# Retention, experts and a max-of-three layer on one core: weight loads, splits and clearing moved between stages

## The chip, the core and the metric

The kernel runs on one core of a Trainium2 chip. The metric is device time in microseconds (us). TensorE is called PE in the rows, VectorE DVE, ScalarE ACT, GpSimd POOL and SyncE SP; SPq and ACTq are the queues from which these engines issue transfers.

## The reference

Retention over 4 batches, 8 heads, 576 positions and 64 dimensions gives 2304 rows of 512 numbers. A gate sends each row to one of 8 experts (1024 wide, capacity 576), whose result is scaled by the gate's weight. A last layer takes the largest of three products and multiplies it by an output matrix.

```python
scores = scale * np.matmul(q, k.transpose(0, 1, 3, 2))
ret = scores * Dmat[None]                      # gamma[h] ** (i - j) for i >= j, else 0
x = np.matmul(ret, v)                          # rows of all heads: [2304, 512]
expert_idx = np.argmax(x @ w_gate, axis=1)     # softmax of the logits gives gate_w
# disp[e, counts[e]] = x[i] for the first `capacity` rows of an expert
h = np.maximum(np.einsum('ecd,edf->ecf', disp, w1), 0.0)
y = np.einsum('ecf,efd->ecd', h, w2)
out[i] = gate_w[i] * y[expert_idx[i], pos[i]]
h = np.maximum(np.maximum(out @ m2_w1, out @ m2_w2), out @ m2_w3)
return h @ w_out
```

## The kernel before

**Three stages.** The program has an order written out by hand; each engine runs its instructions in that order, and semaphores join the engines. The stages are retention with the gate (0 to 133 us of the profile), the eight experts (133 to 373 us) and the last layer.

**Retention.** The 2304 rows go in 20 chunks of 128 rows (every fifth has 64). Step `t` of the loop over chunks works on several chunks at once: PE computes the scores of chunk t+1 (`scores`, L270), turns chunk t-1 and gives its gate logits (`transposes`, L491), adds to the running state (`update`, L295) and computes the outputs of chunk t (`outputs`, L315 and L327). DVE reduces the logits of chunk t-1 (L382 in chunks 0 to 13, L344 later), masks the scores (`cut`, L276), scales the outputs (L336) and the v rows of a chunk two or three ahead (`vprime`, L254). ACT copies the turned rows to a row buffer `xg` (`take`, L389), which frees the one PSUM bank that `transposes` fills. A row buffer waits there for its gate weights. Chunks 0 to 13 are gated in three groups (5, 5, 4): after the group's last chunk `group_choose` picks the experts, `group_place` (PE, L427 on) counts places, and `group_send` scales each row buffer (L483) and writes it to `xd` in DRAM from ACT's queue (L484). Only then is the buffer free; there are seven.

**Loads.** SP issues chunk loads `qk` and `kv` (512 KB each, five and six buffers) up to six chunks ahead, and in the same queue the expert weights (`load_unit`, L138, three buffers `raw` of 512 KB), and at step 4 four writes that put zeros into rows of `xd` (L728). Each transfer that SP or ACT issues takes one of eight completion semaphores in turn; its issue waits until the transfer eight places before it has landed.

**Units.** A unit is 128x1024 weights. `split_hi` (ACT, L144) rounds it to a high part and `split_lo` (DVE, L149) takes the rest; that frees its `raw`. Each expert has eight units: four for the first product (`mm1`), four for the second (`mm2`), one per output block `d`. Before, five units are split in retention (`SPLIT_AT`, high part at the end of that step, low part at the end of the next) and the others in the experts, where `next_split` splits one and loads the next.

**Outputs table.** `spread_otab` (L664) spreads decay factors over partitions by four products with a 0/1 matrix `sel`, which ACT makes first (L702).

**The sum y.** `y` is 128x4x2656 numbers. POOL clears it (L1223 before the first expert, L1092 in the step after its first output block). `mm2` writes each output block into it (ACT, L1144).

## Time and profile before

| what | value |
|---|---|
| median of 3 runs | 668.2 us (661.24 to 670.61) |
| profiled execution | 665.12 us, span 663.1 us, mean granted clock 0.984 |
| PE busy | 634.7 us (96%) |
| DVE busy | 440.1 us (66%) |
| ACT busy | 277.2 us (42%) |
| POOL busy | 215.5 us (33%) |
| bytes moved | 124.05 MB, mean 187 GB/s |

How to read it: PE is busy nearly all the time, so a change pays only where PE waits or runs at the lower of its two clock levels. "Busy" counts a slow matmul as busy, so a stretch with PE at 100% and a granted clock of 0.50 has lost half of its time. The two levels are 2.4 GHz (1.00) and 1.2 GHz (0.50).

### The profile page before, as it was taken

What the parts mean: (1) busy time and instruction counts of PE and PEld (TensorE: products, weight loads), DVE (VectorE), ACT (ScalarE), POOL (GpSimd) and SP (SyncE); (2) the same over time, 40 slices, a digit from 0 to 9 for tenths busy, and PEclk for the clock granted to TensorE, in tenths of its full rate; (3) what the DMA queues carried; (4) which work ended last, traced back from release to release, by engine and by line L of the source; (5) the groups of instructions that cost most, each with busy time, mean ns of one, the idle gap of its engine ahead of it and who ended that gap; (6) DMA issues with size and microseconds to landing.
All of it is one profiled execution on the core that took longest, in us unless ns stands there. A gap on an engine that the chain in (4) does not pass through costs nothing. (4 is left out here: it accounts for less than half of the span.)

```text
span 663.1 us, 12029 instructions
## 1 busy us (share of the span) xinstructions
PE 634.7 (96%) x4523; PEld 596.4 (90%) x4523; DVE 440.1 (66%) x869; ACT 277.2 (42%) x504; POOL 215.5 (33%) x188
## 2 busy tenths in 40 slices
PE   8999989899999999999989999999999999999995
PEld 5888877799999999898979999997899998999983
DVE  3478757774857578689697556577887677446630
ACT  2336324444656565555646543433522225221221
POOL 1001121255655745278885044540210002100011
PEclk8999968999999999999999999999999999999998
DMA  8889952255678787777866324357889641544011
GB/s 280 275 268 324 306 165 104 82 131 184 199 209 223 214 245 208 237 221 239 235 234 207 124 74 136 95 179 263 268 268 316 210 132 49 163 138 146 30 48 50
DMA packets 69876, 124.05 MB, mean 187 GB/s; under 512 B 18506, under 2 KB 41422, under 8 KB 69816
## 3 DMA queue, kind: packets, MB, share of 16 engines
q1 hardware_dynamic: 51896, 94.62, 45.8%
q0 software_dynamic: 15520, 24.50, 12.2%
q10 hardware_dynamic: 2400, 4.14, 1.8%
q8 instruction: 37, 0.61, 0.4%
q14 instruction: 23, 0.19, 0.1%
HBM read 97.27 MB, written 25.91 MB: 186 GB/s over the span
## 5 line engine op out<-in xcount | busy, mean ns | idle before, releaser
L149 DVE TENSOR_TENSOR w<-raw,w 128x1024 fp32r<-128x1024 f32 x72 | 99.9, 1389 | 44.7 <-ACT w L144 44.6
L1138 PE MATMUL b<-h,w 128*128 128x336 f32 (+7 forms) x768 | 118.5, 307 | 3.0 <-DVE h L1114 1.6
L1138 PEld LDWEIGHTS b<-h,w 128*128 128x128 f32 x768 | 109.0, 188 | 5.7 <-DVE h L1114 2.5
L144 ACT ACTIVATE w<-raw 128x1024 fp32r<-128x1024 f32 x72 | 75.9, 1055 | 25.4 <-DMA raw<-in_weights_dram 24.0
L1460 POOL DMA_INDIRECT out_dram<-o,perm_sb x18 | 20.0, 1110 | 192.2 <-ACT o L1458 160.0
L1098 PE MATMUL a<-xt,w 128*128 128x336 f32 (+7 forms) x256 | 77.6, 303 | 0.9 <-DVE xt L196 0.9
L1097 PE MATMUL a<-xt,w 128*128 128x336 f32 (+7 forms) x256 | 77.7, 304 | 0.0
L1099 PE MATMUL a<-xt,w 128*128 128x336 f32 (+7 forms) x256 | 77.3, 302 | 0.0
L187 POOL DMA_INDIRECT who_d<-tok,slots_i x20 | 22.7, 1135 | 100.3 <-DMA who_d<-tok,slots_i 62.2
L1098 PEld LDWEIGHTS a<-xt,w 128*128 128x128 f32 x256 | 48.2, 188 | 1.2 <-DVE xt L196 1.2
L1097 PEld LDWEIGHTS a<-xt,w 128*128 128x128 f32 x256 | 48.1, 188 | 0.5 <-ACT xt L195 0.5
L174 POOL DMA_INDIRECT xr<-xd,who x24 | 37.1, 1547 | 34.8 <-DVE order_w L1159 16.2
L1099 PEld LDWEIGHTS a<-xt,w 128*128 128x128 f32 x256 | 48.1, 188 | 0.0
L1494 PE MATMUL s<-b_ys,w 128*128 128x384 f32 x216 | 40.7, 335 | 1.6 <-ACT p L1524 1.6
L1097 PE MATMUL u<-ys,w 128*128 128x384 f32 x126 | 42.1, 334 | 0.0
L1098 PE MATMUL u<-ys,w 128*128 128x384 f32 x126 | 42.1, 334 | 0.0
L1099 PE MATMUL u<-ys,w 128*128 128x384 f32 x126 | 42.1, 334 | 0.0
L1494 PE MATMUL s<-b_xt,w 128*128 128x384 f32 x216 | 40.4, 334 | 0.0
L1494 PE MATMUL s<-b_h,w 128*128 128x384 f32 x216 | 40.3, 334 | 0.0
L1494 PEld LDWEIGHTS s<-b_ys,w 128*128 128x128 f32 x216 | 37.6, 188 | 2.2 <-ACT p L1524 1.9
L1113 ACT ACTIVATE h<-a 128x336 fp32r<-128x336 f32 (+7 forms) x64 | 26.6, 422 | 29.8 <-PE a L1099 29.6
L1494 PEld LDWEIGHTS s<-b_xt,w 128*128 128x128 f32 x216 | 37.8, 188 | 0.2
(287 smaller groups left out, 1329.1 us busy)
## 6 DMA issues: line engine op xcount, KB each, us to landing
raw<-in_weights_dram SPq DMA_DIRECT2D x64, 512.0 KB, 5.2
w<-sd SPq DMA_DIRECT2D x68, 256.0 KB, 4.1
kv<-in_kv_dram SPq DMA_DIRECT2D x16, 512.0 KB, 5.9
qk<-in_qk_dram SPq DMA_DIRECT2D x15, 512.0 KB, 7.3
d<-in_weights_dram POOLq DMA_DIRECT2D x14, 512.0 KB, 5.9
sd<-y SPq DMA_DIRECT2D x13, 512.0 KB, 3.2
wdec<-mag POOLq DMA_DIRECT2D x16, 256.0 KB, 3.8
raw<-wdec SPq DMA_DIRECT2D x8, 512.0 KB, 3.7
```

Of the source, the lines that this page charges most:

```text
L144: act.activation(out=t[:, 0], in_=raws[w], func=AF.Copy)
L149: engine.tensor_tensor(out=t[:, 1], in0=raws.pop(w), in1=t[:, 0].bitcast(F32), op=ALU.subtract)
L174: pool.indirect_dma_start(out=xr[:n, r, :], out_offset=None, in_=xd[:, :], in_offset=bass.IndirectOffsetOnAxis(ap=who[:n, r, e : e + 1] if ...
L187: pool.indirect_dma_start(out=who_d[:, :], out_offset=bass.IndirectOffsetOnAxis(ap=slots_i[:L, t : t + 1], axis=0), in_=tok[:L, t : t + 1] ...
L1097: pe.matmul(ps, lhsT=wh, rhs=xh, start=first, stop=False)
L1098: pe.matmul(ps, lhsT=wh, rhs=xl, start=False, stop=False)
L1099: pe.matmul(ps, lhsT=wl, rhs=xh, start=False, stop=last)
L1113: act.activation(out=h[:, 0, :wide], in_=ps, func=AF.Relu)
L1138: pe.matmul(ps, lhsT=w[:, a, f * P : (f + 1) * P], rhs=hs[f][:, b, :wide], start=(i == 0), stop=(i == len(todo) - 1),)
L1460: pool.indirect_dma_start(out=out[:, :], out_offset=bass.IndirectOffsetOnAxis(ap=perm_sb[:, g : g + 1], axis=0), in_=o, in_offset=None,)
L1494: pe.matmul(ps, lhsT=a[:, k], rhs=b[:, c], start=first and c == 0 and n == 0, stop=c == 1 and n == 2, skip_group_check=True,)
```

## The change

- Loads: eight units are loaded in retention in both versions. Before, `raw` loads are issued at steps 2, 4 and 5 and behind low parts; now one at each of the steps 2, 3, 5, 6, 7, 10, 11, 12.
- Splits: high parts at steps 4, 6, 7, 8, 9 before, and at 4, 5, 8, 9, 10, 12, 13, 14 now. Eight units, a whole expert, are split in retention, three more than before. The first expert's `mm1` splits one unit instead of three. In the experts 1, 3 and 4 `mm1` splits four units instead of five; the experts 1 and 3 split two behind their last output block.
- Three `raw` loads of the second expert are issued ahead of the first expert's work.
- The zeros of `xd` are written at step 13 instead of 4.
- Eight row buffers `xg` instead of seven, in the room of `sel`. `spread_otab` takes a broadcast column of the identity in `cst` instead, in eight products of 64 columns instead of four of 128.
- ACT clears `y`, one block in each of the steps 0, 2, 8 and 9 of the first expert; POOL clears nothing.

```diff
--- before.py
+++ after.py
@@ -49,9 +49,11 @@
 NCHUNK = len(CHUNKS)
 NPOS = -(-S // P)
 NPATCH = 3
-LOAD_AT = [2, 4, 5]
-SPLIT_AT = [4, 6, 7, 8, 9]
+LOAD_AT = [2, 3, 5, 6, 7, 10, 11, 12]
+SPLIT_AT = [4, 5, 8, 9, 10, 12, 13, 14]
+ZERO_AT = 13
 EARLY_SCATTER = 10
+CLEAR_AT = [0, 2, 8, 9]
 TRANS_AT = [(0, 23), (1, 11), (1, 23), (2, 11)]
 TRANS_FIRST = [(2, 14), (2, 22), (3, 6), (3, 14)]
 GROUPS = [range(0, 5), range(5, 10), range(10, 14)]
@@ -365,7 +367,7 @@
                 dve.reciprocal(out=g[:L], in_=g[:L])
                 ix_t[t], oh_t[t], g_t[t] = ixf, oh, g
                 if NCHUNK - NPATCH <= t < NCHUNK - 1:
-                    xg_t[t] = wk.tile([P, DM], F32, tag="xg", name=f"xg{t}", bufs=7)
+                    xg_t[t] = wk.tile([P, DM], F32, tag="xg", name=f"xg{t}", bufs=8)
                     act.activation(
                         out=xg_t[t][:L].rearrange("p (c n) -> p c n", c=NC), in_=xps_t[t][:L, :, :P], func=AF.Copy
                     )
...
@@ -655,16 +657,18 @@
             dve.memset(ones, 1.0)
 
             decs = st.tile([H, S], F32, name="decs")
-            sel = st.tile([H, NPAIR, 2, D], F32, name="sel")
 
             def spread_otab(j):
                 a, n = j * P, min(P, S - j * P)
                 bank = ps_1.tile([P, DM], F32, tag="po", name=f"spread{j}")
                 for r in range(NPAIR):
-                    pe.matmul(
-                        bank[:, r * n : (r + 1) * n], lhsT=sel[:, r].rearrange("h a d -> h (a d)"),
-                        rhs=decs[:, a : a + n], start=True, stop=True,
-                    )
+                    for par in range(2):
+                        h = 2 * r + par
+                        pe.matmul(
+                            bank[par * D : par * D + D, r * n : (r + 1) * n],
+                            lhsT=ident[:H, h : h + 1].to_broadcast([H, D]),
+                            rhs=decs[:, a : a + n], start=True, stop=True,
+                        )
                 act.activation(
                     out=otab[:, :, a : a + n], in_=bank[:, : NPAIR * n].rearrange("p (r n) -> p r n", r=NPAIR),
                     func=AF.Copy,
@@ -699,11 +703,6 @@
                 skip_group_check=True,
             )
             vprime(1)
-            act.activation(
-                out=sel,
-                in_=ident[:H, :H].rearrange("h (r a) -> h r a", a=2).unsqueeze(3).to_broadcast([H, NPAIR, 2, D]),
-                func=AF.Copy,
-            )
             spread_otab(0)
             for lg_ in lgs:
                 pool.memset(lg_, 0.0)
@@ -720,7 +719,7 @@
                     sp.dma_start(out=cat[:, A_SEQ:], in_=consts[:, C_KEEP + A_SEQ :])
                 if t == 0:
                     act.dma_start(out=who_d.rearrange("(p c) o -> p (c o)", p=P), in_=zero)
-                if t == 4:
+                if t == ZERO_AT:
                     tail = sum(L for _, _, L in CHUNKS[NCHUNK - NPATCH :])
                     blocks = [(0, 1)]
                     blocks += [(r, min(P, 1 + NTOK - r)) for r in range(1 + NTOK - tail, 1 + NTOK, P)]
@@ -797,8 +796,6 @@
                     sent.setdefault(t + 1, []).append(GROUPS[i][j])
                 if t - 1 in SPLIT_AT:
                     split_lo(nxt["split"] - 1, dve)
-                    if nxt["load"] < 8:
-                        next_load()
                 if t < NPOS - 1:
                     spread_otab(t + 1)
                 if t == 0:
@@ -1074,8 +1071,14 @@
         ready = {at - 1: n for n, at in enumerate(slots)}
         slots = {at: n for n, at in enumerate(slots)}
 
+        def clear(c):
+            blank = nc.const_aps.tensor(0.0, [P, NTOK + max(WIDTH)], F32)
+            act.activation(out=y[:, c], in_=blank, func=AF.Copy)
+
         def dec_step(e, k):
             at = e * LAST + k
+            if at in CLEAR_AT:
+                clear(CLEAR_AT.index(at))
             if unsent and at >= LAST and at % 3 == 0:
                 scatter(unsent.pop(0), due=True)
             if (e, k) in finds:
@@ -1087,9 +1090,6 @@
                 decode_top(slots[at + 1])
             if at in slots:
                 decode(slots[at])
-                if slots[at] == 0:
-                    for c in range(NC // 2, NC):
-                        pool.memset(y[:, c], 0.0)
             if at in ready:
                 dec_act(ready[at])
 
@@ -1118,9 +1118,8 @@
                 h_t[e, f] = h
                 if f % 2:
                     units.pop(8 * e + f // 2)
-                if f % 2 or (e in (1, 3, 4) and f == 4):
-                    if (e, f) != (0, 1):
-                        next_split()
+                if f == F // P - 1 or (e and f % 2):
+                    next_split()
                 dec_step(e, f)
 
         def mm2(e):
@@ -1144,7 +1143,8 @@
                 act.activation(out=y[:, d, bass.ds(off, wide)], in_=ps, func=AF.Copy)
                 if e == E - 1:
                     ysplit_part(0, d)
-                next_split()
+                for _ in range(2 if e in (1, 3) and d == NC - 1 else 1):
+                    next_split()
                 dec_step(e, F // P + d)
 
         def scratch(name):
@@ -1218,9 +1218,9 @@
         dec_load(0)
         dec_load(1)
         find_order()
+        for _ in range(3):
+            next_load()
         load_x(1)
-        for c in range(NC // 2):
-            pool.memset(y[:, c], 0.0)
         h2_t, ys_t, m2 = {}, {}, {}
 
         def ysplit_part(i, c):
```

SP's queue around steps 3 to 6 of retention, where the zeros and the raw loads stood (qk, kv: chunk loads; raw: a weight unit), before:

```order
L728 DMA xd_86<-zero_160 4x1x128
L728 DMA xd_86<-zero_160 512x1x128 x2
L728 DMA xd_86<-zero_160 256x1x128
L138 DMA raw1_447<-in_weights_dram 128x1024
L225 DMA qk9_500<-in_qk_dram 128x8x64
L231 DMA kv9_502<-in_kv_dram 64x1024
L138 DMA raw2_504<-in_weights_dram 128x1024
L138 DMA raw3_566<-in_weights_dram 128x1024
L225 DMA qk10_568<-in_qk_dram 128x1024
L231 DMA kv10_570<-in_kv_dram 128x1024
L225 DMA qk11_660<-in_qk_dram 128x1024
```

and now:

```order
L140 DMA raw1_405<-in_weights_dram 128x1024
L227 DMA qk7_455<-in_qk_dram 128x1024
L233 DMA kv7_457<-in_kv_dram 128x1024
L227 DMA qk8_459<-in_qk_dram 128x1024
L233 DMA kv8_461<-in_kv_dram 128x1024
L227 DMA qk9_514<-in_qk_dram 128x8x64
L233 DMA kv9_516<-in_kv_dram 64x1024
L140 DMA raw2_518<-in_weights_dram 128x1024
L227 DMA qk10_582<-in_qk_dram 128x1024
L233 DMA kv10_584<-in_kv_dram 128x1024
L140 DMA raw3_586<-in_weights_dram 128x1024
```

The four zeros are gone from here, and between two raw loads stand one to three chunks' loads; raw2 and raw3 no longer follow each other.

DVE at the end of step 14, between the third group's choice (gids) and the gate of chunk 14 (lg, mx, ix, oh), before:

```order
L414 TENSOR_TENSOR goh_1196<-gsame_1193,gtop_1192 128x32
L415 TENSOR_TENSOR gids_1197<-goh_1196,tab_124 128x64
L344 TENSOR_REDUCE lg_1221<-xps_1216 64x8
L351 MAX mx_1223<-lg_1221 64x8
L353 MAX_INDEX ix_1225<-mx_1223,lg_1221 64x8
L360 CAST ixf_1232<-ix_1225 64x1
L362 TENSOR_SCALAR oh_1234<-cst,ixf_1232 64x8
```

and now:

```order
L416 TENSOR_TENSOR goh_1219<-gsame_1216,gtop_1215 128x32
L417 TENSOR_TENSOR gids_1220<-goh_1219,tab_124 128x64
L151 TENSOR_TENSOR w_1156<-raw_937,w_1156 128x1024
L346 TENSOR_REDUCE lg_1247<-xps_1242 64x8
L353 MAX mx_1249<-lg_1247 64x8
L355 MAX_INDEX ix_1251<-mx_1249,lg_1247 64x8
L362 CAST ixf_1258<-ix_1251 64x1
L364 TENSOR_SCALAR oh_1260<-cst,ixf_1258 64x8
```

One low part (w<-raw,w) has come in ahead of the gate; the same has happened at the ends of steps 13 and 15.

ACT behind the first two output blocks of the first expert (y<-b: an output block; w<-raw: a high part; xt<-tp: the next expert's rows; ISA: register work), before:

```order
L1144 ISA
L1144 ACTIVATE y<-b_0_1992 128x336
L144 ACTIVATE w_2018<-raw_1892 128x1024
L1144 ISA
L1144 ACTIVATE y<-b_1_2032 128x336
L144 ACTIVATE w_2058<-raw_1938 128x1024
L195 ACTIVATE xt_2079<-tp_0_2080 128x352
```

and now:

```order
L1143 ISA
L1143 ACTIVATE y<-b_0_2015 128x336
L146 ACTIVATE w_2041<-raw_1857 128x1024
L1076 ACTIVATE y<-const-float32-0.0 128x2656
L1143 ISA
L1143 ACTIVATE y<-b_1_2054 128x336
L146 ACTIVATE w_2080<-raw_1859 128x1024
L1076 ACTIVATE y<-const-float32-0.0 128x2656
L197 ACTIVATE xt_2102<-tp_0_2103 128x352
```

Behind each of the first two output blocks ACT now clears a block of y; two more clears stand behind the hidden blocks 0 and 2 of `mm1`, and two high parts that stood there are gone.

## Rows read from the trace of the kernel before

In the timelines a row gives start and length in us, engine, line, operation, out<-in, shapes and number, and in brackets the idle time before it and what ended it. In the windows PE, its weight loads, DVE, ACT and POOL stand in that order.

**Rows 1.** The page: granted clock of PE in 40 slices of 16.6 us.

```profile
PEclk8999968999999999999999999999999999999998
```

**Rows 2.** Windows, steps 6, 11, 13, 14, 15: length; engines busy; clock; DMA share; GB/s.

```profile
44.76:50.08 5.32, 5.32 (x70) 4.71 (x69) 4.82 (x20) 2.15 (x5) 0.77 (x1) 1.00 0.79 276
70.85:76.31 5.46, 5.46 (x69) 4.73 (x68) 4.80 (x20) 2.14 (x5) 0.78 (x1) 1.00 1.01 352
79.63:86.58 6.95, 4.94 (x56) 4.18 (x56) 2.54 (x6) 1.92 (x3) 0.90 (x1) 0.94 1.04 365
86.58:94.89 8.31, 8.31 (x74) 7.74 (x76) 3.60 (x13) 1.58 (x4) 1.92 (x2) 0.50 0.57 168
94.89:102.42 7.53, 6.51 (x94) 5.53 (x91) 6.61 (x31) 2.76 (x7) 1.95 (x2) 0.93 0.10 21
```

**Rows 3.** Windows, three stretches of low clock, then one of transfers.

```profile
10.30:14.10 3.80, 3.80 (x48) 3.32 (x44) 1.89 (x3) 1.21 (x4) 0.00 (x0) 0.55 1.09 379
84.80:95.90 11.10, 10.87 (x99) 9.93 (x99) 4.66 (x19) 2.94 (x9) 1.92 (x2) 0.54 0.60 194
105.90:109.70 3.80, 3.79 (x24) 3.33 (x24) 2.72 (x10) 2.13 (x3) 0.00 (x0) 0.55 0.35 137
46.00:90.00 44.00, 39.83 (x513) 35.33 (x511) 32.59 (x85) 20.31 (x36) 5.75 (x5) 0.95 1.02 323
```

**Rows 4.** Timeline, PE in retention: start, length, instruction, idle before and releaser.

```profile
8.87 1.15 PE L664 MATMUL spread<-decs,sel 8*128 8x128 f32 x8 [1.07 <-ACT sel L702]
...
45.40 1.09 PE L327 MATMUL o<-pt,vp 128*64 128x128 f32 x16
...
58.31 1.19 PE L491 MATMUL xps<-idw,xT 128*128 128x136 f32 x8 [0.94 <-ACT xg L389]
...
69.57 0.17 PE L433 MATMUL gpo<-goh,tri 128*128 128x8 bf16 x1 [0.93 <-DVE goh L414]
...
85.03 1.51 PE L491 MATMUL xps<-idw,xT 128*128 128x136 f32 x8 [2.01 <-ACT xg L389]
```

**Rows 5.** Timeline, ACT in retention.

```profile
8.19 0.63 ACT L702 ACTIVATE sel<-cst 8x512 f32<-8x512 f32 x1 [5.95 <-DMA cst<-in_consts_dram]
...
84.38 0.60 ACT L389 ACTIVATE xg<-xps 128x512 f32<-128x512 f32 x1 [3.94 <-DMA xd<-xg]
```

**Rows 6.** Timeline, DVE in retention.

```profile
67.68 0.69 DVE L254 TENSOR_TENSOR vp<-kv,cat 128x512 f32<-128x512 f32 x1 [0.91 <-DMA kv<-in_kv_dram]
...
83.99 0.69 DVE L254 TENSOR_TENSOR vp<-kv,cat 128x512 f32<-128x512 f32 x1 [1.74 <-DMA kv<-in_kv_dram]
```

**Rows 7.** Timeline, SP's queue, step 5 of retention.

```profile
37.66 7.54 SPq L138 DMA_DIRECT2D raw<-in_weights_dram  x2
```

**Rows 8.** Waits of SP's queue in retention: us in total, times, longest.

```profile
SPq L231 <- DMA xd<-xg: 8.6, 2, 6.5
```

**Rows 9.** Timeline, PE in experts 0 to 4, its waits that the change touches.

```profile
166.62 0.43 PE L1098 MATMUL a<-xt,w 128*128 128x352 f32 x1 [0.91 <-DVE xt L196]
...
243.05 2.13 PE L1138 MATMUL b<-h,w 128*128 128x308 f32 x12 [0.58 <-ACT h L1113]
...
273.50 2.21 PE L1138 MATMUL b<-h,w 128*128 128x296 f32 x12 [0.87 <-ACT h L1113]
```

**Rows 10.** Timeline, POOL and ACT in experts 0 and 4.

```profile
161.09 4.61 POOL L1092 MEMSET y<- 128x2656 f32 x2
...
163.48 0.45 ACT L1144 ACTIVATE y<-b 128x336 f32 x1 [3.14 <-POOL y L1092]
...
268.16 1.06 ACT L144 ACTIVATE w<-raw 128x1024 fp32r<-128x1024 f32 x1 [3.48 <-DMA raw<-in_weights_dram]
```

**Rows 11.** Groups of instructions in retention: xcount, busy us, mean ns, idle before.

```profile
L149 DVE TENSOR_TENSOR w<-raw,w 128x1024 fp32r<-128x1024 f32 x5 | 6.1, 1215 | 0.0
...
L144 ACT ACTIVATE w<-raw 128x1024 fp32r<-128x1024 f32 x5 | 5.3, 1057 | 2.8 <-ACT xg L483 1.4 <-DMA raw<-in_weights_dram 1.4
```

**Rows 12.** The page: output blocks of the experts, 24 matmuls each.

```profile
L1138 PE MATMUL b<-h,w 128*128 128x336 f32 (+7 forms) x768 | 118.5, 307 | 3.0 <-DVE h L1114 1.6
```

More of the change, by code (lines that the diff above doesn't have):

```diff
@@ L387, in take @@
                 )
-                xg_t[t] = wk.tile([P, DM], F32, tag="xg", name=f"xg{t}", bufs=7)
+                xg_t[t] = wk.tile([P, DM], F32, tag="xg", name=f"xg{t}", bufs=8)
                 act.activation(
@@ L519, in gate2 @@
                 xps = xps_t.pop(t)[:L, :, :P]
-                xg = xg_t.pop(t) if t in xg_t else wk.tile([P, DM], F32, tag="xg", name=f"xg{t}", bufs=7)
+                xg = xg_t.pop(t) if t in xg_t else wk.tile([P, DM], F32, tag="xg", name=f"xg{t}", bufs=8)
                 if t < NCHUNK - NPATCH:
```

## The prediction

> **What bounds the kernel now.** I read the page first: PE is busy in 96% of the span, and its granted clock is well below full in two slices, 83 to 116 us, and a little in the first and the last [rows 1]. So a gain has to come from places where PE waits, or from a stretch at 1.2 GHz. Then I cut retention into windows by step, and the low stretches by themselves [rows 2, 3], and took PE's waits from its timeline, one by one [rows 4, 9]. For each wait I followed the releaser: to ACT [rows 5, 10], from there to a transfer or to POOL, and for late transfers to SP's queue [rows 6 to 8].
>
> What the reader is to see: in steps 6 and 11 PE is busy throughout, with DVE at 4.8 of 5.3 to 5.5 us close behind it. Step 13 takes 6.95 us with PE idle for 2.0 of them; the idle time is the wait at 85.03, ahead of `transposes`, for ACT's copy into a row buffer, and that copy waited 3.94 us for a row buffer's write to DRAM to land [rows 2, 4, 5]. Behind it PE falls to 1.2 GHz for 11.1 us and step 14 takes 8.31 us at a clock of 0.50, PE busy all the time [rows 2, 3]. From 133 us on the experts keep PE full but for a few waits of 0.6 to 0.9 us [rows 9].
>
> **The change, part by part.** Durations are of the profiled execution, 665.1 us (span 663.1 and 2.0 around it).
>
> 1. *No `sel`.* The first spread waits 1.07 us for `sel`, which ACT makes in 0.63 us once the constants have landed at 8.19 [rows 4, 5]. The constants are still needed, so 0.6 us goes. The spread itself becomes eight products of 64 columns. Bounds: the outputs' 64-column products come in pairs and take 1.09 us for 16 rows of the trace, the full-width spread 1.15 us for 8 [rows 4], so the price is nil; if the pairs ran one behind the other it would be 1.15 us more, five times at most, 5.5 us. I take nil, since the output products write the same two halves of the bank. **-0.6 us.**
>
> 2. *Eight row buffers.* Chunk 7 needs an eighth buffer before chunk 0's has landed in DRAM, chunk 12 before chunk 5's. The waits of 0.94 us at 58.31 and of 2.01 us at 85.03 end there [rows 4]. What is late next at 85: DVE waits 1.74 us for `kv` until 83.99 [rows 6]. That one goes only if item 3 holds. **-0.9 and -2.0 us.**
>
> 3. *Loads one by one.* SP's queue stood 7.54 us on two `raw` loads in a row, the second waiting for the low part that frees its buffer [rows 7]; now each load comes at a step whose buffer was freed the step before. In the same queue a `kv` load stood up to 6.5 us behind a row write [rows 8], through the eight semaphores in turn; with the zeros gone from there, the place eight before it is a chunk load. Afterwards the transfers ran full, DMA share 1.02 at 323 GB/s from 46 to 90 us [rows 3], catching up. So `kv` for steps 10 and 13 should land sooner, and DVE's wait of 0.91 us at 67.68, which is PE's wait of 0.93 us at 69.57 [rows 4, 6], goes. **-0.9 us** (0 if transfers stay behind). The zeros at step 13 have only chunk 19's loads behind them in SP's queue, first used by `vprime` at step 16; cost nil, and if that cover were gone, a wait like the 1.74 us for a late `kv` [rows 6].
>
> 4. *The splits.* A low part costs DVE 1.22 us, a high part ACT 1.06 us [rows 11]. ACT has room, busy for at most 2.76 us in the steps shown [rows 2]. DVE has little. Step 6 gains a low part: 4.82 + 1.22 = 6.0 us against 5.32, 0.7 over; the steps behind it lose theirs, so PE, which works ahead, loses part: **+0.5** (0 to 0.7). Step 11: 4.80 + 1.22 = 6.0 against 5.46: **+0.55** (0 to 1.22). Step 13: 2.54 + 1.22, below PE's 4.94: nil. Step 15: 6.61 + 1.22 = 7.8 us against 7.53, DVE is the bound: **+0.6** (0.3 to 1.22).
>
> 5. *Step 14 at full clock.* If the wait at 85 goes, PE need not fall to 1.2 GHz. Its 8.31 us at 0.50 are 4.2 us at 1.00; DVE has 3.60 + 1.22 = 4.8 us in that step, and its idle 4.7 us, spent on a slow PE, would be 2.35 at full clock [rows 2]: between 4.8 and 7.2 us. I take 5.7, below the middle, since the low part falls into that idle time: **-2.6 us** (0 if the clock falls all the same; -4.1 if PE alone sets it).
>
> 6. *Clearing y on ACT.* POOL's second pair of clears takes 4.61 us and holds ACT's output block back for 3.14 us, and so the next expert's rows: PE waits 0.91 us at 166.62 [rows 9, 10]. ACT's clear is not in the trace. Bounds: 2.3 us (half of POOL's 4.61) and 2.75 us (2656 columns at the 1057 ns for 1024 of a high part [rows 11]). From 0.63 us for 512 and 1.06 for 1024 it is 0.83 ns a column and 2.4 us for 2656 [rows 5, 11]. Behind an output block ACT then has 0.45 + 1.06 + 2.4 = 3.9 us in the 3.7 us that PE needs for a block (118.5 us by 32) [rows 10, 12]. It slips 0.2 us a block, twice. The clears in `mm1` stand where two high parts stood, and PE has six banks to write ahead. Queued behind the last clear are the copies of the next expert's rows; PE needs the last of them three blocks later than the first. **-0.9 us** (0 to -0.9).
>
> 7. *Experts 3 and 4.* The waits of 0.58 and 0.87 us at the start of `mm2` [rows 9] come from ACT standing on a `raw` that has not landed, 3.48 us in expert 4 [rows 10], with the hidden blocks behind it. The fifth split in `mm1` was what ran out of loads; it moves behind the last output block, where PE has banks to write ahead. **-1.4 us** (0 to -1.45). In expert 0 the two high parts that leave were hidden under PE: nil.
>
> Sum: -0.6 -0.9 -2.0 -0.9 +0.5 +0.55 +0.6 -2.6 -0.9 -1.4 = **-7.7 us**, 657.4 against 665.1. The median of the runs shown is 668.2, 3.1 us above the profiled execution, and the lowest is 661.24, so runs differ by more than most terms here. I add half of the 3.1: **659 us** for the median.
>
> **The rivals.**
>
> *The loads stay behind, and the clock still falls.* For it: transfers run at a share of 1.0 over 44 us [rows 3], and items 2, 3 and 5 need them earlier. The clock fell also at 105.9, with no single wait of 2 us but a step behind it in which PE was busy for 6.51 of 7.53 us [rows 2, 3]. The Trainium skill (TensorE: Matmul & The Clock Gate, section "A second HAM failure mode: psum-queue depth-cycling") says that frequent short idles between groups of matmuls are enough to make the clock swing; the fall at 105.9 agrees with it. By that rule, low parts that leave PE idle for a moment in steps 13 to 15 keep a low stretch there. Time: items 3 and 5 give nothing, the wait at 85 shrinks by 1.0 only, the rest stands: -0.6 -0.9 -1.0 +0.5 +0.55 +0.6 -2.3 = -3.2, **662 us**, 663 to 665 for the median.
>
> *Nothing is given back, and all low stretches go.* The low parts hide and the starts at 10.3 and 105.9 run at 2.4 GHz too (3.8 us each, 1.9 back; of the 11.1 us half, 5.5 [rows 3]): -2.5 -0.9 -2.0 -0.9 -5.5 -1.9 -2.3 = -16.0, **649 us**, 651 for the median. Against it: DVE's sums in item 4.
>
> *Slower: the low clock comes earlier and stays.* If the low part in step 11 leaves PE idle by about 2 us within a step, as ahead of 84.8, the clock falls there. Steps 11 to 15 took 31.6 us from 70.85 to 102.42; at 1.2 GHz each takes what step 14 took, 8.31 us [rows 2]: 41.6, +10.0 us. With items 1, the first wait of 2, step 6, 6 and 7 left (-0.6 -0.9 +0.5 -2.3), **671.8 us**, and about 674 for the median. Against it: 0.55 us over in that step is a quarter of the 2 us from which it decides.
>
> **How the numbers follow.** Chances: forecast 0.50, loads and clock 0.30, everything gone 0.15, slower 0.05. The range goes from the second rival's median, 651, over the forecast to the first rival with the median's full 3.1 us and the 2 us by which the slowest run lies above the median: **651 to 667 us**. Two per cent, about what a measurement of this kernel can tell from no change, is 13.4 us of 668.2: under 654.8 lies the second rival and the edge of the forecast's bounds, so faster 0.17; slower than 681.6 needs the last rival to last beyond step 15, 0.03; within, 0.80.
>
> **What would show it.** Right: no wait of PE for ACT's row copy at `transposes` in steps 8 to 14; the `kv` scaling of DVE without a transfer wait in steps 10 and 13; a granted clock of 1.00 over step 14; the gate of chunk 14 starting some 6 to 7 us earlier than 94.89; PE without the waits at the start of expert 1 and of `mm2` in the experts 3 and 4. Wrong: DVE busy without a gap over steps 11 to 15 and PE waiting for it; a stretch of 0.50 anywhere from 70 to 105 us that is as long as before; PE waiting for the next expert's rows behind ACT's clears; a spread that takes twice its 1.15 us.

## The result: 0.9% slower, where 1.4% less was forecast

| | before | changed |
|---|---|---|
| median (22 runs each) | 662.69 us (657.68 to 670.61) | 668.11 us (662.78 to 671.72) |
| profiled execution | 665.12 us, span 663.1 us | 671.05 us, span 669.2 us |
| mean granted clock in it | 0.984 | 0.981 |

The ratio is **1.0086, 95% interval 1.0064 to 1.0109**: 5 to 6 us slower. The forecast was 659 us, range 651 to 667; median and sign are both off. The base moved too: with 22 runs the kernel before has its median at 662.69 us, 2.4 us below its profiled execution; the prediction had seen a median 3.1 us above it and counted on half of that.

### The profile page after: what moved, and what is told of

Read it like the earlier page. It is cut to its first block, busy times and chain, and to the rows that moved or that the text cites. A ratio compares the mean times of both kernels' runs of the same rounds, so it can differ in the third digit from the quotient of the medians.

```text
span 669.2 us, 12112 instructions
## 1 busy us (share of the span) xinstructions
PE 635.9 (95%) x4563; PEld 596.3 (89%) x4563; DVE 438.7 (66%) x869; ACT 284.2 (42%) x507; POOL 201.7 (30%) x184
## 3 DMA queue, kind: packets, MB, share of 16 engines
q0 software_dynamic: 15520, 24.50, 12.1%
## 5 line engine op out<-in xcount | busy, mean ns | idle before, releaser
L1137 PE MATMUL b<-h,w 128*128 128x336 f32 (+7 forms) x768 | 123.2, 314 | 7.5 <-DVE h L1114 5.7
L1137 PEld LDWEIGHTS b<-h,w 128*128 128x128 f32 x768 | 112.2, 193 | 11.6 <-DVE h L1114 7.6
L146 ACT ACTIVATE w<-raw 128x1024 fp32r<-128x1024 f32 x72 | 75.8, 1056 | 27.6 <-DMA raw<-in_weights_dram 25.2
L1494 PE MATMUL s<-b_ys,w 128*128 128x384 f32 x216 | 40.6, 335 | 3.3 <-ACT p L1524 3.3
L1038 POOL TENSOR_TENSOR d<-d,top 128x512 f32<-128x512 f32 x16 | 21.4, 1337 | 67.0 <-DVE top L1035 26.4
L1494 PEld LDWEIGHTS s<-b_ys,w 128*128 128x128 f32 x216 | 37.7, 188 | 3.7 <-ACT p L1524 3.7
L1494 PE MATMUL s<-b_xt,w 128*128 128x384 f32 x216 | 40.4, 334 | 0.0
L1494 PE MATMUL s<-b_h,w 128*128 128x384 f32 x216 | 40.3, 334 | 0.0
L1524 ACT ACTIVATE p<-s 128x384 f32<-128x384 f32 x18 | 8.8, 492 | 68.5 <-PE s L1494 58.7
```

The lines of the kernel that those rows point to most:

```text
L146: act.activation(out=t[:, 0], in_=raws[w], func=AF.Copy)
L1038: pool.tensor_tensor(out=low, in0=low, in1=top.bitcast(F32), op=ALU.mult)
L1137: pe.matmul(ps, lhsT=w[:, a, f * P : (f + 1) * P], rhs=hs[f][:, b, :wide], start=(i == 0), stop=(i == len(todo) - 1),)
L1494: pe.matmul(ps, lhsT=a[:, k], rhs=b[:, c], start=first and c == 0 and n == 0, stop=c == 1 and n == 2, skip_group_check=True,)
```

## The profile after

The two profiles, cut at the first product of each stage (differences of PE's start times):

| stretch | before | changed | difference |
|---|---|---|---|
| start to expert 0 | 133.24 | 128.57 | -4.67 |
| experts 0 and 1 | 64.51 | 62.99 | -1.52 |
| experts 2 to 6 | 149.76 | 159.33 | **+9.57** |
| expert 7 to the first `s` products (L1494) | 124.51 | 125.89 | +1.38 |
| from there to the end | 191.1 | 192.4 | +1.3 |

So in these two profiles retention and the clears brought 6.2 us, near the forecast's 6.3 for them, and the experts 2 to 6 took 9.6. That the 6.2 meets the forecast is luck, as a second profile of before shows below. Windows of `mm2` of the experts 4 and 6, first of before, then of the changed kernel, where `mm1` of expert 4 stands ahead (the columns are those of [rows 2]):

```profile
270.58:288.03 17.45, 16.49 (x110) 14.74 (x109) 14.25 (x31) 10.52 (x18) 5.15 (x5) 1.00 0.71 241
329.99:347.51 17.52, 15.52 (x110) 13.90 (x109) 17.02 (x19) 8.10 (x15) 14.56 (x13) 1.00 0.67 223
```

```profile
251.41:266.30 14.89, 13.22 (x99) 12.98 (x97) 6.42 (x10) 6.86 (x12) 1.26 (x2) 1.00 0.67 175
266.30:286.76 20.46, 18.28 (x109) 16.20 (x109) 17.21 (x35) 9.69 (x18) 12.31 (x11) 0.92 0.70 223
329.86:350.89 21.03, 18.17 (x111) 16.28 (x109) 14.65 (x19) 9.15 (x16) 14.35 (x14) 0.84 0.61 210
```

Both `mm2` took 17.5 us at full clock; now 20.5 and 21.0, with the clock at 0.92 and 0.84. What is missing to 1 there comes to 5.0 us, so about half of the 9.6 is the lower clock (an estimate); most of the rest is PE's waits. Where PE stood, from its timeline in expert 4 (start, duration, and in brackets the idle time ahead with its releaser), against the one wait of 0.87 us in `mm2` of expert 4 in [rows 9] (the 0.58 us there belongs to expert 3):

```profile
266.30 3.25 PE L1137 MATMUL b<-h,w 128*128 128x296 f32 x20 [1.67 <-DVE h L1114]
270.27 0.78 PE L1137 MATMUL b<-h,w 128*128 128x296 f32 x2 [0.72 <-DVE h L1114]
272.50 0.78 PE L1137 MATMUL b<-h,w 128*128 128x296 f32 x2 [1.46 <-DVE h L1114]
```

A hidden block `h` is written by ACT first and then, with ACT's part as an input, by DVE. DVE's come late because ACT's do. ACT's timeline there, against the 3.48 us of [rows 10]:

```profile
251.99 1.05 ACT L146 ACTIVATE w<-raw 128x1024 fp32r<-128x1024 f32 x1
253.70 1.06 ACT L146 ACTIVATE w<-raw 128x1024 fp32r<-128x1024 f32 x1 [0.65 <-DMA raw<-in_weights_dram]
254.66 0.71 ACT L1113 ACTIVATE h<-a 128x296 fp32r<-128x296 f32 x2
262.49 1.06 ACT L146 ACTIVATE w<-raw 128x1024 fp32r<-128x1024 f32 x1 [7.12 <-DMA raw<-in_weights_dram]
```

The first two are the pair behind expert 3's last block. They use up what had landed. The next high part, behind f = 1, stands 7.12 us on its `raw`, with the hidden blocks f = 2 to 7 queued behind it. That load went out at 251.96 and landed 10.5 us later; the page gives 4.8 us as the median of all loads. What was in flight with it is in POOL's timeline, the gather of expert 5's rows by index:

```profile
248.08 1.71 POOL L176 DMA_INDIRECT xr<-xd,who  x1 [0.30 <-issue]
250.09 1.66 POOL L176 DMA_INDIRECT xr<-xd,who  x1 [0.30 <-DVE step L1201]
252.05 0.92 POOL L176 DMA_INDIRECT xr<-xd,who  x1 [0.30 <-issue]
```

From 250 to 290 us such a gather takes 15.1 us to land in the median.

Slow loads and ACT's waits for them are not new. In the profile of before, loads issued about 2 to 6 us behind a gather's start land after 6.8 to 10.2 us too, and over the whole kernel ACT stands on loads for nearly as long:

```profile
L144 ACT ACTIVATE w<-raw 128x1024 fp32r<-128x1024 f32 x72 | 75.9, 1055 | 25.4 <-DMA raw<-in_weights_dram 24.0
```

What the change moved is where the wait falls. In before's expert 4, ACT came to such a load at 264.7 us, 7.2 us into `mm1`, and stood 3.48 us, with four hidden blocks still to write. Now it comes 4.0 us into `mm1`, with six.

Behind PE's waits the clock fell; the windows of that stretch:

```profile
266.30:274.50 8.20, 6.02 (x33) 4.78 (x34) 8.13 (x12) 4.96 (x11) 4.68 (x4) 1.00 0.59 191
274.50:278.00 3.50, 3.50 (x16) 3.08 (x15) 3.44 (x6) 1.29 (x2) 0.16 (x1) 0.51 1.00 289
```

The Trainium skill (DMA: Bandwidth & Descriptors, section "Queues, rings and completion order") says that each DMA engine takes turns between the queues it has work for, packet by packet. The trace fits this, without showing single packets: the load, in SP's queue, landed at 262.46, the gather's first part, in POOL's, at 262.97; both were slow together.

Groups of the page of the changed kernel, ACT's high parts and PE's `mm2` (busy, mean ns, idle ahead). Before, the latter had 118.5 us and waits of 3.0 [rows 12]; PE's waits grew by 4.5 us, ACT's for loads by 1.2:

```profile
L146 ACT ACTIVATE w<-raw 128x1024 fp32r<-128x1024 f32 x72 | 75.8, 1056 | 27.6 <-DMA raw<-in_weights_dram 25.2
L1137 PE MATMUL b<-h,w 128*128 128x336 f32 (+7 forms) x768 | 123.2, 314 | 7.5 <-DVE h L1114 5.7
```

In retention, windows that answer to the first and last stretch of [rows 3] and to steps 14 and 15 of [rows 2]:

```profile
10.30:14.10 3.80, 3.80 (x76) 3.27 (x75) 2.87 (x5) 1.68 (x4) 0.00 (x0) 1.00 1.07 348
46.00:90.00 44.00, 40.23 (x538) 35.79 (x538) 34.01 (x86) 22.06 (x38) 8.10 (x6) 0.96 0.96 281
84.69:90.36 5.67, 5.67 (x99) 5.20 (x97) 4.62 (x14) 2.62 (x6) 0.91 (x1) 1.00 1.02 375
90.36:99.14 8.78, 6.22 (x65) 5.31 (x62) 7.82 (x33) 3.48 (x8) 1.94 (x3) 0.81 0.60 121
```

Step 14 took 5.67 us at full clock, as forecast (5.7). But 3.11 us are lost at step 10, where DVE waits for a `kv`, against 0.91 us in [rows 6], and 1.3 us in step 15:

```profile
66.61 0.69 DVE L256 TENSOR_TENSOR vp<-kv,cat 128x512 f32<-128x512 f32 x1 [3.11 <-DMA kv<-in_kv_dram]
```

## The experiments

Ratios are to the kernel before, timed on the same chip in the same call, with 95% intervals.

### The experts' order of splits

**Order back.** The changed kernel with before's order in the experts.

```diff
-                if f == F // P - 1 or (e and f % 2):
+                if (e and f % 2) or (e in (1, 3, 4) and f == 4):
...
-                for _ in range(2 if e in (1, 3) and d == NC - 1 else 1):
-                    next_split()
+                next_split()
```

> The changed kernel with the experts' splits where the kernel before has them: in expert 0 none in mm1, in experts 1, 3 and 4 a fifth one behind f = 4, and one, not two, behind the last block of mm2. Theory A (the loads' reserve): the split moved behind the last block is taken out of the three landed loads just as the gather of the next expert's rows starts; the load that it triggers goes into the gather, lands in 10.5 us in place of about 4, and ACT stands on it in the next mm1 for 5.6 to 7.1 us, with the hidden blocks behind it. Then mm2 of experts 2, 4 and 6 come back to 15.4, 17.5 and 17.5 us, the 4.7 us of retention and the 1.5 us of expert 0's clear stay: about 6 us below the kernel before, ratio 0.991 (0.987 to 0.995). Theory B (POOL, freed of the clears, issues the gathers earlier against PE, whatever the splits' order): mm2 of experts 4 to 6 stay long, ratio 1.003 to 1.009. Theory C (the last layer's 2.7 us are the change's): they stay here in either case, ratio 0.995 under A.

Measured 1.0047 (1.0022 to 1.0072): 0.4% of the 0.9% goes with the order. The 6 us below before didn't come: `mm2` of experts 2 and 4 is back at 15.4 and 17.1 us, but that of 3 and 6 takes 18.4 and 20.4, and retention gave nothing on average (below). Experts 2 to 6 take 153.6 us in its profile, 5.7 less than changed and still 3.8 more than before, so the order is not all of the 9.6.

**Order alone.** The kernel before with the one move.

```diff
-                if f % 2 or (e in (1, 3, 4) and f == 4):
+                if f % 2 or (e in (4,) and f == 4):
...
-                next_split()
+                for _ in range(2 if e in (1, 3) and d == NC - 1 else 1):
+                    next_split()
```

> The kernel before with one move alone: the fifth split of experts 1 and 3 goes from behind f = 4 to behind the last block of mm2 (expert 4 keeps its own). Theory A: ACT stands 5 us or more on a weight load in mm1 of expert 2 and 4, in place of 1.0 and 3.5; mm2(4) grows by 2 to 5 us and the clock falls there; 2 to 6 us slower than before, ratio 1.003 to 1.009. Theory B: the same as before, 0.998 to 1.002. The on-record step 7: 1.4 us faster, 0.998.

Measured **1.0074 (1.0039 to 1.0109)**, theory A's size. With the kernel before otherwise unedited, this shows that the move costs time. `mm2` of expert 4 takes 22.2 us, and ACT's timeline shows the stall of the changed kernel:

```profile
252.05 0.80 ACT L1113 ACTIVATE h<-a 128x296 fp32r<-128x296 f32 x2
259.01 1.06 ACT L144 ACTIVATE w<-raw 128x1024 fp32r<-128x1024 f32 x1 [6.16 <-DMA raw<-in_weights_dram]
```

**Without the gathers.** Both kernels with plain row blocks for the experts 2 to 7. These experts then get other rows, in the same number; the selection by index is what is left out.

```diff
-            pool.indirect_dma_start(
+            if e < 2:
+                pool.indirect_dma_start(
...
+            else:
+                pool.dma_start(out=xr[:n, r, :], in_=xd[e * 256 + r * RP : e * 256 + r * RP + n, :])
```

> The changed kernel with the rows of experts 2 to 7 read from DRAM as plain blocks by POOL's queue, in place of the gather by index (so these experts get other rows; nothing else is left out). Theory A (a weight load issued behind the gather lands in about 10 us, and the new order asks for one more there): the loads land in 3 to 6 us throughout, ACT stands on none for over 2 us in experts 2 to 6, PE's waits at the start of mm2 and the low clock behind them go; it loses no more than 0 to 2 us to the same edit of the kernel before (retention's part less the clears'), against 5.7 us for the two kernels themselves. Ratio to the kernel before 0.988 to 0.996. Theory B (the new order costs by what it puts on ACT and DVE, wherever the loads are): it stays 4 to 6 us above the same edit of the kernel before.

> The kernel before with the same edit: plain blocks in place of the gathers of experts 2 to 7 (other rows; nothing else is left out). Theory A: PE's waits of 0.5 to 1.0 us in mm2 of experts 3 to 6, some 5 us in all, mostly go: ratio 0.988 to 0.995. Theory B: 0.997 to 1.000.

Measured 0.9968 (0.9933 to 1.0002) and 1.0014 (0.9975 to 1.0054). With the gathers out of the way the changed kernel no longer loses: it goes from 0.9% slower to level or a little faster, so its loss needs them. The test takes the whole change, not the order alone. The high part that stood 7.12 us now stands 1.55:

```profile
260.67 1.06 ACT L146 ACTIVATE w<-raw 128x1024 fp32r<-128x1024 f32 x1 [1.55 <-DMA raw<-in_weights_dram]
```

ACT's groups, changed and before, against 25.2 and 24.0 us of waits above:

```profile
L146 ACT ACTIVATE w<-raw 128x1024 fp32r<-128x1024 f32 x72 | 75.8, 1055 | 10.9 <-DMA raw<-in_weights_dram 8.9
```

```profile
L144 ACT ACTIVATE w<-raw 128x1024 fp32r<-128x1024 f32 x72 | 75.8, 1054 | 9.0 <-DMA raw<-in_weights_dram 6.8
```

Theory A of the second expectation fell all the same: before's waits went, experts 2 to 6 took 145.0 us in its profile against 149.8, and its median didn't move. Against the first profile of before, it gave 1.1 us back ahead of expert 2 and 3.2 behind expert 6; why its median stayed is open.

**Early pairs, and early pairs from expert 1.** The changed kernel with two splits behind blocks 0 and 1 of `mm2`, ahead of the gather, and fewer in `mm1`. The diff is of the second; the first also has pairs in expert 0.

```diff
-                if f == F // P - 1 or (e and f % 2):
+                if f == F // P - 1 or (e and f == F // P - 3) or (e in (1, E - 1) and f % 2):
...
-                for _ in range(2 if e in (1, 3) and d == NC - 1 else 1):
+                for _ in range(2 if d < 2 and 0 < e < E - 1 else 1):
```

> The changed kernel with the experts' splits moved out of the gather's time: in mm1 behind f = 5 and 7 only, in mm2 two behind each of the blocks 0 and 1 and one behind 2 and 3. Theory A: from the gather's issue to its landing 12 to 16 us later three splits are asked for, as many as there are landed loads, so ACT stands on a load for under 2 us anywhere in experts 2 to 6 and PE's waits at the start of mm2 go, the kernel before's 3 us of them too: 7 to 11 us below the kernel before, ratio 0.984 to 0.990. Theory B: the splits' order does not matter: 1.003 to 1.009. A third way: pairs of low parts hold DVE's rows for the next expert back in mm2, where DVE is the busiest: 0.995 to 1.000.

> The changed kernel with the splits of experts 1 to 6 out of the gather's time, as in the run with early pairs (behind f = 5 and 7, two behind each of the blocks 0 and 1, one behind 2 and 3), but expert 0's blocks with one split each, so that its loads don't meet the gather of expert 1's rows, and the two that are missing behind f = 1 and 3 of expert 1. Theory A: the 2.9 us wait for expert 1's rows and the low clock behind it (4.65 us longer mm2 in expert 0) go: 4 to 5 us faster than the early pairs, ratio 0.991 to 0.994. If that wait was a matter of the single profile and not of the order: 0.998 to 1.000, as there.

Measured 0.9996 (0.9955 to 1.0036) and **0.9958 (0.9925 to 0.9991)**. Against the changed kernel that is 0.9 and 1.3%. In the first PE waited 2.90 us at 159.07 for expert 1's rows. The gather was not late there, as the second expectation has it: ACT had a clear of 2.40 us behind the high parts of a block, and the copies of those rows stood behind both. The second has no such wait. In the second ACT's waits for weights are 12.1 us from 125 to 375 us, where the changed kernel has 25.2 and before 22.6, and PE waits 1.0 us for hidden blocks there, against 7.5 and 3.0. Still, `mm2` of expert 6 took 19.8 us, with a low stretch.

### Clearing y

**POOL clears in the changed kernel; ACT clears in the kernel before** (the diff of the second; the first is its reverse).

```diff
+            if at in CLEAR_AT:
+                clear(CLEAR_AT.index(at))
...
-                if slots[at] == 0:
-                    for c in range(NC // 2, NC):
-                        pool.memset(y[:, c], 0.0)
...
```

> The changed kernel with y cleared on POOL again, as before. Theory A: the wait of 0.9 us for expert 1's rows is back and nothing else moves: 0.9 to 1.5 us slower than the changed kernel, ratio to the kernel before 1.010 to 1.011. Theory B: the gathers come later again, the stalls of experts 4 to 6 shrink and it beats the changed kernel by 5 us or more, ratio 0.998 to 1.002.

> The kernel before with y cleared on ScalarE at the change's four places, and nothing else. On record: 0.9 us, ratio 0.9986. By the two profiles of before and after: expert 1's mm1 from 16.9 to 15.4 us, 0.9977. By the run with POOL's clears against the changed kernel: 3.7 us, 0.9945.

Measured 1.0142 (1.0097 to 1.0188) and 0.9977 (0.9942 to 1.0012). Both point to a gain; the direct one is 1.5 us and its interval takes in zero. In every profile `mm1` of expert 1 is 15.4 to 15.5 us with ACT's clears and 16.8 to 17.5 with POOL's. Theory B fell: with POOL's clears the changed kernel is slower, and its experts 2 to 6 take 161.4 us. The group of ACT's clears in the changed kernel:

```profile
L1076 ACT ACTIVATE y<-const-float32-0.0 128x2656 f32<-128x2656 f32 x4 | 9.7, 2416 | 0.0
```

### Retention

**Retention alone, and before once more.** The first is the changed kernel with before's order of splits and POOL's clears; the second has no edit.

> The changed retention alone (no sel, eight row buffers, loads, splits and zeros at the new steps); the experts' splits and the clearing of y on POOL are those of the kernel before. Theory R (retention gains what the two profiles say, 4.7 us up to the first expert's matmuls): 3 to 6 us faster, ratio 0.991 to 0.996. Theory S (the profiled run of the kernel before had a slow retention, with three low stretches of the clock; in the run with the old retention and one other order of splits the experts start at 125.8 us, in three with the new one at 125.9 to 130.8): retention as a whole gives nothing, the 2.3 us that it leads at chunk 14 go in steps 15 and 16 with their longer DVE and in the end: 0.997 to 1.006. Adding up the medians (1.0086 whole, 0.4% of it the splits' order, clears that gain 0.5%) would make it 1.009.

> The kernel before once more, for a second profile of it. Theory S: the experts start near 126 to 129 us, not at 133.24, with one or two low stretches of the clock in retention; theory R: at 132 to 134 again.

Measured **1.0042 (1.0002 to 1.0081)**: theory S. The second profile of before starts its experts at 124.79 us, 8.5 us earlier than the one that the prediction rested on, with a span of 655.7 us. Its windows for the low stretches of [rows 3]:

```profile
10.30:14.10 3.80, 3.80 (x64) 3.39 (x66) 2.49 (x4) 1.59 (x5) 0.00 (x0) 1.00 1.08 374
84.80:95.90 11.10, 9.65 (x120) 8.46 (x120) 9.80 (x46) 3.71 (x9) 2.88 (x3) 0.85 0.44 126
105.90:109.70 3.80, 3.80 (x53) 3.29 (x51) 2.56 (x17) 1.41 (x5) 1.61 (x2) 1.00 0.19 69
```

No dip at 10 us, none at 106 (there is one of 3.4 us at 114), 0.85 in place of 0.54 around 90, and no wait for a row buffer at chunk 12. Six profiles with the old retention start the experts at 133.2, 124.8, 125.8, 124.5, 126.4 and 133.7 us; seven with the new one at 125.9 to 131.8, median 128.6, where the six have 126.1. The lead of 4.7 us was that of one profile. What the new one loses always, at full clock, is seen in DVE's scaling of the outputs of chunks 14, 15 and 16 (timelines of before again, then of retention alone):

```profile
84.78 0.42 DVE L336 TENSOR_TENSOR xT<-o,otab 128x256 f32<-128x256 f32 x1 [0.88 <-PE o L327]
91.07 0.69 DVE L336 TENSOR_TENSOR xT<-o,otab 128x512 f32<-128x512 f32 x1
98.69 0.68 DVE L336 TENSOR_TENSOR xT<-o,otab 128x512 f32<-128x512 f32 x1
```

```profile
83.95 0.42 DVE L338 TENSOR_TENSOR xT<-o,otab 128x256 f32<-128x256 f32 x1 [0.87 <-PE o L329]
91.55 0.69 DVE L338 TENSOR_TENSOR xT<-o,otab 128x512 f32<-128x512 f32 x1 [0.30 <-PE o L329]
99.58 0.68 DVE L338 TENSOR_TENSOR xT<-o,otab 128x512 f32<-128x512 f32 x1
```

From chunk 14 to 16 before takes 13.9 us, the new retention 15.6, and a lead of 0.8 us becomes 0.9 behind. Over the profiles it is 13.7 to 13.9 us with the old retention, the first one with its low clock apart, and 15.2 to 15.8 with the new one.

**Seven splits, six splits.** Retention alone without its last, or its last two low parts.

```diff
-SPLIT_AT = [4, 5, 8, 9, 10, 12, 13, 14]
+SPLIT_AT = [4, 5, 8, 9, 10, 12]
...
-                if (e and f % 2) or (e in (1, 3, 4) and f == 4):
+                if (e, f) in ((0, 5), (0, 7)) or (e and f % 2) or (e in (1, 3, 4) and f == 4):
```

> The changed retention alone, as run above, but without the low part in step 15: the eighth unit is split in expert 0, behind f = 7 of mm1. If the low part of that step is what retention loses (step 15 took 7.2 to 7.7 us with it and 6.1 to 6.3 without, step 16 8.0 and 7.6, PE's wait for DVE's hit 2.56 and 1.45): step 15 back to 6.1 to 6.3, step 16 to 7.6, the gather of expert 0's rows issued 1.5 us earlier, ratio 0.998 to 1.002 against 1.004. If step 15 stays over 7 us the low part is not its cause; if it comes back and the ratio stays at 1.004, the end of retention, behind that gather, decides.

> The changed retention alone, without its last two low parts (units 6 and 7, split in expert 0 behind f = 5 and 7 of mm1): six units split in retention. Theory P (the low parts in the stage where DVE is the bound): from chunk 14 to 16 PE-side time is back from 15.2 to 15.8 us to the 13.7 of five of six profiles with the old retention, PE's wait for the hit at chunk 14 from 2.56 to 1.45 us, the gather of expert 0's rows goes out 1.6 us earlier, and the median falls by 2 to 4 us: ratio 0.998 to 1.001 against 1.004. Theory Q (the end of retention, its wait for those rows and the low clock there, is the loss, however the low parts stand): the stretch is back to 13.7, the ratio stays 1.003 to 1.006.

Measured 1.0043 (1.0002 to 1.0084) and 1.0014 (0.9979 to 1.0048). The first of the two expectations had the stretches one off: the last low part is in the one from chunk 15 to 16, and without it that is 7.64 us again (from 8.03); the one before it holds the seventh low part and stayed at 7.77. Without both, chunk 14 to 16 takes 13.7 us and PE's wait for `ghit` (DVE's work on the third group, the hit of the expectation) is back from 2.56 to 1.44 us, as theory P has it. The traces settle that these two low parts cost 1.5 to 2.1 us there. That they are what the median loses is not shown: the two intervals overlap, and taking out `sel`, which the new retention also does, measures as much by itself (below).

**Zeros early.** Retention alone with the zeros at step 4.

```diff
-ZERO_AT = 13
+ZERO_AT = 4
```

> The changed retention alone, with the zeros of the row table stored at step 4 again. If the zeros at step 13 (four stores in SP's queue for 5 us, a DMA share of 1.0 from 84 to 91 us) hold transfers back that the end of retention waits for: 2 to 4 us less, ratio 0.997 to 1.001. If they are free there, as the prediction has it: 1.003 to 1.006, or worse by a late load at steps 5 to 9 (up to 1.008).

Measured 1.0104 (1.0040 to 1.0168), where retention alone had 1.0042 (1.0002 to 1.0081). Late zeros cost nothing that shows; that they are a gain is not shown, since the intervals overlap.

**Rows alone, seven buffers, no sel.** Items 1 and 2 on the kernel before; retention alone with seven row buffers (the diff, one of three places); item 1 on the kernel before.

```diff
-                    xg_t[t] = wk.tile([P, DM], F32, tag="xg", name=f"xg{t}", bufs=8)
+                    xg_t[t] = wk.tile([P, DM], F32, tag="xg", name=f"xg{t}", bufs=7)
...
```

> Eight row buffers and no sel, the steps of loads, splits and zeros those of the kernel before, everything else too: items 1 and 2 of the prediction alone. On record: 0.6 + 0.9 + 2.0 us and the clock's 2.6 behind the last, ratio 0.991 to 0.995. By the six profiles with the old retention, where the wait ahead of the transposes at chunk 12 was 2.0, 0, 1.7, 0, about 1 and 2.9 us: 1 to 2 us on average, 0.996 to 0.999. If the buffers only swap that wait for a late kv load: 0.999 to 1.002.

> The changed retention alone, with seven row buffers as before (no sel, new steps of loads, splits and zeros stay). Theory V (the eighth buffer sends chunk 7's rows to DRAM ahead of the loads of chunks 13 to 15, and kv 13 lands late: the wait of 2 to 3 us at step 10 that the runs with eight buffers had in five of nine profiles): no wait over 1 us for kv at step 10, the short wait for a row buffer at chunk 7 is back, ratio 0.998 to 1.002 against 1.004 with eight. If the step-10 wait has nothing to do with the buffers: 1.003 to 1.007, and waits for buffers on top.

> The kernel before without sel alone, spread as 64-column products (step 1 of the prediction). On record 0.6 us: 0.999. By the start of the profiles (chunk 0 at 12.6 to 14.4 us in either kernel): nothing, 0.998 to 1.002. With the run of items 1 and 2 together at 1.005 it tells the eighth buffer's part: 0.3 to 0.6% if this one is at 1.000.

Measured 1.0049 (1.0014 to 1.0083), 1.0008 (0.9980 to 1.0036) and **1.0051 (1.0019 to 1.0084)**. So items 1 and 2 do not gain 3.5 us, they lose 3, and item 1 by itself loses as much. The eighth buffer takes away the waits for a buffer in all eleven profiles that have it, but 1.9 to 3.1 us of waiting for `kv` at step 10 stand in five of the eleven profiles with eight, against 0 to 1.5 with seven. With seven in the new retention it was 1.12 us and the ratio 0.3% lower, within the intervals.

Where item 1 loses is seen in part. With before's order of splits in the experts, experts 2 to 6 take 149.8, 151.2 and 151.6 us in the three profiles that have `sel` and 149.7 to 156.6 in the eight that don't (mean 154.0; 154.4 with that edit alone), though nothing of the experts was edited. The order alone, with `sel`, has 154.3. It may be no fixed price: the run with seven buffers has no `sel` either and measured 1.0008. Why the experts take longer is open; so the 9.6 us of the changed profile are only in part the order's.

### A version that beats both

Old retention, ACT's clears (as above, not in the diff), and the splits out of the gather's time; then the same with the zeros at step 13.

```diff
-                if f % 2 or (e in (1, 3, 4) and f == 4):
-                    if (e, f) != (0, 1):
-                        next_split()
+                if f in (5, 7) or (f == 3 and e in (0, 1, 2, 7)) or (f == 1 and e in (1, 7)):
+                    next_split()
...
-                next_split()
+                for _ in range(2 if d < 2 and 0 < e < E - 1 else 1):
+                    next_split()
```

> The retention of the kernel before, y cleared on ACT as the change has it, and the experts' splits out of the gather's time (in experts 1 to 6 two behind each of the blocks 0 and 1 of mm2, in mm1 behind f = 5 and 7, with f = 1 or 3 as well in experts 0, 1, 2 and 7 to keep count). If the parts add up (retention alone costs 0.4%, clears give 0.2%, the pairs with the changed retention and the clears 0.4% below before): 0.6 to 1.0% below the kernel before, ratio 0.990 to 0.994. If the pairs only repaired the new order: 0.996 to 0.999.

> The best kernel so far (retention of the kernel before, y cleared on ACT, the experts' splits out of the gather's time; 0.9917) with the zeros at step 13, as the change has them. The run with the changed retention and early zeros was 0.6% slower than the one with late zeros: if that holds here, 0.985 to 0.990; if the late zeros only helped where the loads stood elsewhere, 0.990 to 0.994.

Measured 0.9917 (0.9884 to 0.9950) and **0.9896 (0.9852 to 0.9939)**, 658.14 us against 665.43 in that call. In the profile of the first, its fastest run, experts 2 to 6 take 145.6 us, in that of the second 148.9 (149.8 before, 159.3 changed). ACT still stands on loads for 20.0 us over the whole of the first, so the sum of these waits does not tell the kernels apart. The late zeros fit their 0.2%, but the two intervals overlap.

## Why the prediction was wrong

- **Item 7 (experts 3 and 4, -1.4 us) failed, in sign.** "It moves behind the last output block, where PE has banks to write ahead" looked at PE's room and not at the loads. A high part there takes a landed load at the moment the gather starts, and the next load lands in 10.5 us, so ACT stands on it early in `mm1`, ahead of hidden blocks that PE needs. Alone it costs 0.74%, undone it gives 0.4% back: 3 to 5 us. Experts 2 to 6 lost 9.6 us in the profile, about half of it low clock and part of it not the order's. The 3.48 us for which ACT stood on a `raw` [rows 10] held the sign: it was short of a landed load, and the item asked for one more, earlier.
- **Items 2, 3 and 5 rested on one profile of a stretch that varies.** The wait of 2.01 us at 85.03 and the 11 us at 1.2 GHz behind it [rows 3, 4] were absent in the second profile of before, and the experts started 8.5 us earlier. Of the six profiles with the old retention four have that wait (1.65 to 2.94 us), but only in the first is the low stretch behind it longer than 3.4 us. The terms of 2.0 and 2.6 us fit that one execution (step 14 took 5.67 us) and not the kernel's median. Item 3's `kv` wait grew from 0.91 to 3.11 us at step 10 in the changed profile.
- **Item 1 (-0.6) failed, in sign.** The product price was right: a spread takes 1.09 us of PE's time, 1.15 before. But chunk 0 is scaled no earlier (12.5 to 14.4 us in most profiles of either kind), and the edit by itself measured +0.5%, 3.4 us. The item looked at the first spread alone; what the profile of that edit shows is longer experts 2 to 6, and the cause of that stays open.
- **Item 4 was mis-sized at one place.** Step 15's +0.6 measured 0.4; the low part ahead of it, that "falls into that idle time" in item 5, costs 1.1 us (7.2 us from chunk 14 to 15 against 6.1). The forecast had that low part for nothing, in an idle time read while PE ran at the lower clock.
- **Item 6 was right in mechanism:** 2.4 us a clear, measured 2.416; PE's wait at the start of expert 1 gone, 1.5 us of `mm1` where 0.9 were forecast. In the median the clears alone measured 0.2%, with zero inside the interval.
- **The rivals.** The first had the loads behind, but in retention and with a gain. The slower one had a fall of the clock in steps 11 to 15; there was one in step 11 and one in step 15, of 3.4 us each, and neither stayed. Its condition, a wait of about 2 us, was not met where the clock fell in expert 4: the waits there were 1.67, 0.72 and 1.46 us. None looked at the loads in the experts.
- **The base** was put at 666.7 us (665.1 and half of 3.1), 4.0 above the median of 22 runs, since three runs and one profile stood for the kernel.

The parts measured alone are +0.4 (retention, with item 1 in it), -0.2 (clears) and +0.7% (order), together +0.9, the whole. Each has an interval of 0.35 to 0.4% to either side, so that they meet so closely is partly luck.

## What to carry to other kernels

Where a work item is moved, count how many landed inputs it leaves for the items behind it until the next slow transfer has passed; an idle consumer is not room if the buffers are empty. Profile a kernel more than once before pricing a wait or a low-clock stretch in it: here a single profile of the same program stood 7 us from the next.

## What was not expected of the hardware

- A 512 KB weight load issued about 2 to 6 us behind the start of a gather of 272 to 352 rows by index took 6.8 to 10.2 us in the profile of before and 8.6 to 10.5 in the changed one, against medians of 5.2 and 4.8 us over all loads. With plain row blocks ACT's waits for loads fall from 24.0 to 6.8 and from 25.2 to 8.9 us.
- One program's clock differs from run to run: in the stretch before the experts the old retention had 3.4 to 17 us at 1.2 GHz, the new one 6.8 to 17. Over the timed runs the mean granted clock is 0.982 for the changed kernel and, in the later measurements, 0.986 to 0.988 for the kernel before: span times what is missing to 1 is 12.0 us against 7.7 to 9.4.
- Taking out `sel`, used in the first 32 us alone, goes with a slower last layer: from the first `s` product to the next output product (L1478) seven profiles with `sel` take 67.4 to 68.1 us, thirteen without it 67.8 to 72.4 (mean 69.9). The run with that edit alone has 68.5, 0.8 more than the mean with `sel`, so by its profile most of the 0.5% is not lost there. In that stage the third scatter of output rows is issued 1.6 us later in nine of the thirteen, and ACT and PE wait for its buffer: in the changed kernel, against a wait of 1.57 us before,

```profile
484.46 1.32 PE L1494 MATMUL s<-b_ys,w 128*128 128x384 f32 x6 [3.33 <-ACT p L1524]
```

No instruction of that stage differs. What links the two is open, and nothing was tried that could tell.
